# A fused attention and bilinear feed-forward kernel: first weights by narrower columns, first batch's units in another order

## The chip, the cores and the metric

The kernel runs on one core of a Trainium2 chip. The metric is the device time of one execution in microseconds (us), the median of several runs. The profile is one execution recorded by the hardware profiler, which names for every instruction its engine, its line, its tiles, its start and its length.

## What is computed

Attention over 32 memory slots per head, then a feed-forward layer without a nonlinearity, in which two projections are multiplied element by element:

```
# q, k, v: 8 x 8 x 576 x 64 (batch, head, token, dim); phi: 8 x 8 x 576 x 32
a      = softmax(phi over the tokens)
k_m    = einsum('bhsm,bhsd->bhmd', a, k)      # 32 x 64 per head
v_m    = einsum('bhsm,bhsd->bhmd', a, v)
attn   = softmax(q @ k_m.T / 8 over the 32 slots) @ v_m
x      = attn, heads side by side             # 4608 tokens x 512
out    = ((x @ w_a) * (x @ w_b)) @ w_out      # w_a, w_b: 512 x 1536, w_out: 1536 x 512
```

All inputs and the output are float32 in memory. The kernel computes in float16 with float32 accumulation.

## The kernel before

The kernel never forms `x`. It multiplies v_m into the weights first (a **fold**: `vab` = v_m @ w_a and v_m @ w_b, per batch), and then multiplies the attention weights `A` (8 heads x 32 slots = 256 rows, as two groups g of 128, over 576 tokens) by `vab`. An **up** of one block i of 128 features and one half of the tokens (288) is `up_half`: two matmuls for `pa` (line 593, x = 0), evicted by ScalarE into `a_sb` (line 601), and two for `pb`, which VectorE multiplies by `a_sb` into `ht` (line 604). A **down** multiplies `ht` by `w_out` (line 390 for the first four token blocks, afterwards two token blocks at a time with seven products on sums of blocks, line 465, whose weight sums GpSimd forms in `sum_weights`).

The schedule is written out by hand. `units(b)` gives for each batch b a dictionary of named steps, and strings list the order in which they are issued; every engine then works through its own instructions in that order. The names that matter:

- `exp0 exp1`: exp of phi on ScalarE, two halves. `qt0` to `qt3`: transposes of q on VectorE, line 204.
- `ks0 ks1`: sums of k over the tokens on TensorE (line 256), by group, with a normalised copy on VectorE; `vs0 vs1` the same for v; `kt`, `vt`: their transposes (line 274, copy at 277).
- `s0 s1`: scores (line 293); `e0 e1`: their exp (line 306); `den0 den1`: denominators as a product with block-wise ones (line 315) and Ln on ScalarE (line 316), in two token halves; `nr0 nr1`: exp(-Ln) and the multiply into `A` (lines 324, 326).
- `v0a x0a`: a fold of 512 columns with `w_a` (line 338) and its casts to float16 (line 350, one by ScalarE, one by VectorE); `v0b x0b` the same with `w_b`; `hv..`, `hx..`: the same with 256 columns.
- `a3`, `b3`: ups of feature block 3 (`pa`, `pb`), both token halves; `a3.0` only the first half.
- `y3`: three steps of the early downs (`early_downs`: 48 products of 512 columns; four token blocks by thirds of the 12 feature blocks). `f4`: four products of a zero tile (`fill`, line 151) of 256 columns; their result is used by nobody, they keep TensorE at work.
- `-`: nothing; `L`: the loads of the batch after next; a prime: the next batch; an underscore: the batch before.

`chain(0, ...)` at lines 682 to 685 is the first batch's attention and ups, `chain(1, ...)` (line 686) the second batch's attention with early downs between its steps. The later batches run from `slots` strings: one entry after each half of an up step.

All loads but that of the first k go out on GpSimd's queue (software descriptors) and are cast to float16 on the way, except phi and the first k. A load on this queue waits until the eighth before it has landed, so GpSimd stands in the issue order; the transfers follow in that order. The order before is: phi, q (two halves) and v of batch 0, `w_a` and `w_b` in three blocks of 512 columns each, first third of `w_out`, phi, k and half of q of batch 1, second third of `w_out`, the other half of q, v in two halves, last third of `w_out`, and then batches 2 to 4.

Of the kernel before, what the change touches and what calls it, by code (L numbers as in the profile page):

```python
# [8 lines left out]
F32 = mybir.dt.float32  # L9
# [4 lines left out]
P = 128  # L14
CS = 16.0
# [3 lines left out]
def kernel(  # L19
# [11 lines left out]
    nc = tc.nc  # L31

    B, H, S, D = q.shape
# [4 lines left out]
    NFF = d_ff // P  # L38
# [8 lines left out]
    small = ctx.enter_context(tc.tile_pool(name="small", bufs=2))  # L47
# [26 lines left out]
    kv_sbs = [consts.tile([P, 3, NHP, NI * D], F16, name=f"kv_sb{t}") for t in range(2)]  # L74

    def load_phi(b):
        phis[b] = inp.tile([P, NHP, NI * M], F32, name="phi_sb")
        nc.gpsimd.dma_start(out=phis[b], in_=rows(phi, b))

    def load_k(b, hps=slice(0, NHP)):  # L80
        kvs[b] = kv_sbs[b % 2]
        nc.gpsimd.dma_start(out=kvs[b][:, 0, hps], in_=rows(k, b)[:, hps])

    def load_v(b, hps=slice(0, NHP)):
        nc.gpsimd.dma_start(out=kvs[b][:, 1, hps], in_=rows(v, b)[:, hps])

    def load_q(b, hps=slice(0, NHP)):
        if b not in qs:
            qs[b] = inp.tile([P, NHP, NI * D], F16, name="q_sb")
        nc.gpsimd.dma_start(out=qs[b][:, hps], in_=rows(q, b)[:, hps])  # L90

    def load(b):
        load_phi(b)
        load_k(b)
        load_v(b)
        load_q(b)

    def load_wab(lo, hi):
        nc.gpsimd.dma_start(out=wa_sb[:, :, lo:hi], in_=wa_rows[:, :, lo:hi])
        nc.gpsimd.dma_start(out=wb_sb[:, :, lo:hi], in_=wb_rows[:, :, lo:hi])  # L100

    def load_wo(n):
        sl = slice(4 * n, 4 * (n + 1))
        nc.gpsimd.dma_start(out=wo_sb[:, sl, :], in_=wo_rows[:, sl, :])


# [2 lines left out]
    halves = [slice(0, 2), slice(2, 4)]  # L109
# [37 lines left out]
    def fill(n, cols=512):  # L147

        pw = banks.tile([P, 512], F32, name="pw")
        for _ in range(n):  # L150
            nc.tensor.matmul(pw[:, :cols], warm[:, :P], warm[:, :cols], start=True, stop=True)  # L151
# [3 lines left out]
    nc.vector.memset(kv_sbs[0][:, 2], 1.0 / CS)  # L155
    for x in halves:
        nc.vector.tensor_copy(out=kvs[0][:, 0, x], in_=k_f32[:, x])
    load_wab(0, 512)

    ones = consts.tile([P, 4, 32], F16, name="ones")  # L160
    nc.vector.memset(ones, 1.0)
# [2 lines left out]
    nc.gpsimd.affine_select(out=ones, in_=ones, compare_op=ALU.is_ge, fill=0.0, base=31,  # L164
                            pattern=[[32, 4], [0, 32]], channel_multiplier=-1)
    load_wab(512, 1024)
    load_wab(1024, 1536)
    load_wo(0)
    load_phi(1)
    load_k(1)  # L170
    load_q(1, halves[0])
    load_wo(1)
    load_q(1, halves[1])
    for x in halves:
        load_v(1, x)
    load_wo(2)
    nc.gpsimd.memset(kv_sbs[1][:, 2], 1.0 / CS)

    attn = {}
    vabs = {}  # L180
# [6 lines left out]
    def units(b):  # L187

        u = {}
        t = {}  # L190
# [115 lines left out]
                nc.scalar.activation(out=Ev[:, g, :, z, :], in_=pss, func=AF.Exp, scale=1.0 / (8.0 * CS))  # L306
                banks.free(bank)

        def denominators(g):

            t["L", g] = small.tile([P, S], F32, name="L")
            for hf in range(2):
                sl = slice(HALF * hf, HALF * (hf + 1))
                pD = banks.tile([P, HALF], F32, name="pD")
                nc.tensor.matmul(pD, ones, t["E"][:, g, sl], start=True, stop=True)  # L315
                nc.scalar.activation(out=t["L", g][:, sl], in_=pD, func=AF.Ln)  # L316
# [36 lines left out]
        def one(f, *a):  # L353
            return lambda: f(*a)

        for z in range(2):
            u[f"exp{z}"] = one(exp_phi, z)
            u[f"ks{z}"] = one(sums, z, 0)
            u[f"kt{z}"] = one(transpose, z, 0)
            u[f"vs{z}"] = one(sums, z, 1)  # L360
            u[f"vt{z}"] = one(transpose, z, 1)
            u[f"s{z}"] = one(scores, (z,))
            u[f"e{z}"] = one(exp_scores, z)
            u[f"den{z}"] = one(denominators, z)
            u[f"nr{z}"] = one(normalise, z)
            for hf in range(2):
                u[f"nr{z}{hf}"] = one(normalise, z, slice(hf, hf + 1))
            for n in range(NCH):
                u[f"v{n}{'ab'[z]}"] = one(fold, 512 * n, 512 * (n + 1), (z,))
                u[f"x{n}{'ab'[z]}"] = one(take_fold, 512 * n, 512 * (n + 1), z)  # L370
            for n in range(2):
                u[f"hv{n}{'ab'[z]}"] = one(fold, 256 * n, 256 * (n + 1), (z,))
                u[f"hx{n}{'ab'[z]}"] = one(take_fold, 256 * n, 256 * (n + 1), z)
# [13 lines left out]
    def down_part(po, bank, cidx, lo, hi):  # L387
        pair, c = divmod(cidx, NI)
        for i in range(lo, hi):
            nc.tensor.matmul(po, ht[:, i, P * c:P * (c + 1)], wo_sb[:, i, :],  # L390
                             start=(i == 0), stop=(i == NFF - 1))
            if i == NFF - 1:
                banks.free(bank)
                o_sb = opool.tile([P, d_model], F32, name="o_sb")
                nc.scalar.mul(out=o_sb, in_=po, mul=1.0 / (CS * CS))
                for z in range(2):
                    slot = 2 * c + z
                    nc.sync.dma_start(out=out_rows[2 * pair + slot // NI, slot % NI],
                                      in_=o_sb[64 * z:64 * z + 64, :])
            yield  # L400
# [8 lines left out]
    def early_downs():  # L409

        pos = [banks.take([P, d_model], F32, "po", hold=True) for c in range(EARLY)]
        for n in range(3):
            for c in range(EARLY):
                yield from down_part(*pos[c], c, 4 * n, 4 * (n + 1))

# [197 lines left out]
    def ups(steps, side=()):  # L615

        side = iter(side)
        for step in steps:
            for _ in up(*step):
                work.advance()  # L620
                next(side, us[step[0]]["-"])()
        for f in side:
            work.advance()
            f()

    def steps(b, lo, hi):

        return [(b, i, (0, 1)) for i in range(lo, hi)]

    def half_steps(b, hf, lo=0):  # L630

        return [(b, i, (hf,)) for i in range(lo, NFF)]
# [10 lines left out]
    def slots(b, names):  # L643

        def both(fs):
            return lambda: [f() for f in fs]
        def unit(n):
            if n == "fin":
                return lambda: work.pull(-work.done % NFF)
            if n == "L":  # L650
                return lambda: load(b + 2) if b + 2 < B else None
            if n[0] == "y":
                return lambda: some(int(n[1:]))
            if n[0] == "d" and n[1:].isdigit():
                return lambda: work.pull(int(n[1:]))
            return us[b + n.endswith("'") - n.endswith("_")][n.rstrip("'_")]

        return [both([unit(n) for n in x.split("+")]) for x in names.split()]
# [3 lines left out]
    def some(n):  # L662
        for _ in range(n):
            next(early, None)

    def chain(b, plan):


        for x in plan.split():
            if x[0] == "f":  # L670
                fill(int(x[1:]), 256)
            elif x[0] == "y":
                some(int(x[1:]))
            elif x[0] in "ab":
                i, _, hf = x[1:].partition(".")
                for h in ([int(hf)] if hf else (0, 1)):
                    up_half(b, int(i), h, "ab".index(x[0]))
            else:
                us[b][x]()

    fill(16)
    chain(0, "exp0 exp1 qt0 qt1 f12 ks0 f4 kt0 f2 ks1 f1 s0 e0 kt1 qt2 qt3 f2 den0 f4 s1 e1 nr0 f8 vs0 vs1 den1 f2 vt0 vt1 nr1 f4")
    chain(0, "v0a x0a f4 a0 a1 v0b x0b f4 b0 b1 a2 b2 v1a x1a a3 b3 a4 a5 v1b x1b a6 a7 b4 b5 v2a x2a b6 b7 a8 a9")
    load(2)
    chain(0, "v2b x2b a10 a11 b8 b9 b10 b11")
    chain(1, "exp0 y1 exp1 y11 ks0 ks1 y1 qt0 y3 kt0 qt1 s0 e0 kt1 y6 qt2 qt3 den0 y3 s1 nr0 y4 vs0 e1 vs1 den1 y1 vt1 y2 vt0 nr1 hv0a hx0a hv0b y2 hx0b y3")
    load(3)
    sum_weights()
    ups(steps(1, 0, 4), slots(1, "- hv1a+hx1a hv1b+hx1b+y1 - v1a+x1a y3+v1b x1b y3"))
    ups(half_steps(1, 0, 4), slots(1, "- v2a+x2a+v2b+x2b+qt0' - - qt1'+exp0'+qt2' exp1' - kv'+km'+y9"))  # L690
    work.plan(S + HALF, 10)
    ups(half_steps(1, 1, 4), slots(2, "qt3 kvt - sc+e0+e1 - den0+den1+nr0 - v0+nr1+x0a x0b - v1+x1b x1a"))
    second = "v2_+x2a_+exp0 x2b_ exp1 - kv+km qt0 kvt+qt1 - qt2+qt3 sc+e0 e1+v0+x0a den0+x0b nr0+v1+x1a L x1b+exp0' - exp1' v2+x2a den1+qt0' x2b - nr1+qt1'+kv'+km' - - qt2'+kvt'+qt3'"
    every = "- sc+e0 e1 den0 v0+x0a+x0b - - nr0+exp0' - - v1+x1a qt0' x1b+den1 exp1' - v2+x2a+x2b nr1+qt1' kv'+km' qt2' - qt3' - kvt'+L -"
    last = "sc+e0 - e1 - v0+x0b - x0a den1 - - den0 v1+x1b x1a+nr0 - - - - nr1+v2+x2a - - - - - x2b"
    for b in range(2, B):
# [37 lines left out]
```

The softmax here doesn't subtract the row's maximum and nothing guards it: scores larger than these inputs give would overflow.

## Time and profile before

| | |
|---|---|
| time, median of 3 runs | 244.36 us (243.72 to 244.43) |
| profiled span | 241.9 us, granted clock 0.998 |
| busy: VectorE, ScalarE, GpSimd | 167.1, 157.0, 155.9 us |
| loads and stores | 34.12 MB in 24660 packets, mean 141 GB/s |
| exp of phi of batch 0 starts | 7.72 us |
| last up of batch 0 ends, first down starts | 34.4 us |
| first up of batch 1 starts | 48.44 us |

The profile's page gives for each engine the busy time and its share of the span, and then the span in 40 slices of about 6 us, each with a digit for the busy share in tenths. For a stretch of the span, the profile can list the busy time of TensorE (PE), its weight loads (PEld), VectorE (DVE), ScalarE (ACT) and GpSimd (POOL), each with the count of instructions, and then the granted TensorE clock, the DMA share and the GB/s moved. In the timeline each row is one group of like instructions: start, length, engine, line, what it writes and reads, how many, and in square brackets how long the engine stood idle before it and what ended that. In the list of loads the last number is the time from issue to landing.

### The profile page before, as it was taken

The page shows a single profiled execution, that of the slowest core. Times are in us where ns is not written, and L with a number is a line of the kernel's source. Part 1 is how long each engine was busy: PE and PEld are TensorE (multiplying, and loading weights), DVE is VectorE, ACT ScalarE, POOL GpSimd, SP SyncE. Part 2 cuts the span into 40 slices and gives each one's busy share as a digit, 9 for nine tenths or more (in the row PEclk, how much of TensorE's full clock was granted, in tenths as well). Part 3 has the DMA queues.
Part 4 walks back from the last instruction along what each step waited for, and adds up shares of the span by engine and source line. Part 5 has one row for each costly group of instructions (what it writes and reads, how often), then busy time and mean ns, then how long its engine had stood idle before and what let it go on. Part 6 is the DMA issues. An engine that isn't in the chain of part 4 may idle for free.

```text
span 241.9 us, 7661 instructions
## 1 busy us (share of the span) xinstructions
PE 232.9 (96%) x3043; PEld 167.8 (69%) x3043; DVE 167.1 (69%) x402; ACT 157.0 (65%) x406; POOL 155.9 (64%) x130
## 2 busy tenths in 40 slices
PE   7889999999999999999999999999999999999993
PEld 2555664356757867777788777877787878888882
DVE  4536784478858868976984659875987586756642
ACT  2265761679597599598757777587856877465430
POOL 7822354499879549873989759882939087936001
PEclk9999999999999999999999999999999999999999
DMA  6999999999948938962279632795210303033154
GB/s 232 236 206 207 208 255 208 259 223 281 221 98 187 219 81 170 239 117 44 46 176 210 143 87 56 176 205 136 49 43 13 80 13 76 12 80 67 40 128 118
DMA packets 24660, 34.12 MB, mean 141 GB/s; under 512 B 1936, under 2 KB 18704, under 8 KB 24624
## 3 DMA queue, kind: packets, MB, share of 16 engines
q0 software_dynamic: 18160, 23.14, 51.1%
q1 hardware_dynamic: 5952, 9.70, 15.8%
q10 hardware_dynamic: 512, 0.79, 1.0%
q8 instruction: 24, 0.39, 0.6%
q14 instruction: 12, 0.10, 0.1%
HBM read 42.47 MB, written 9.44 MB: 215 GB/s over the span
## 4 chain that ended last, share of the span: by engine, by line
PE 88%; ACT 3%; DMA 3%; DVE 2%; issue 1%; POOL 0%; DVEq 0%; POOLq 0%
PE pa L593 20%; PE pb L593 19%; PE py L465 17%; PE pv L465 8%; PE pva L338 5%; PE po L390 5%; PE px L465 4%; DMA q_sb<-in_q_dram 3%; PE pkv L213 2%; PE pscore L293 2%; PE pD L315 2%; PE pk L256 1%; ACT E L306 1%; PE pT L242 1%; PE pw L151 1%
## 5 line engine op out<-in xcount | busy, mean ns | idle before, releaser
L604 DVE TENSOR_TENSOR ht<-a_sb,pb 128x288 f16<-128x288 f16 x168 | 73.2, 448 | 37.8 <-ACT a_sb L601 28.6
L593 PEld LDWEIGHTS <-vab 128*128 128x128 f16 x768 | 71.7, 98 | 27.1 <-issue 9.4
L601 ACT CAST a_sb<-pa 128x288 f16<-128x288 f32 x168 | 66.7, 408 | 26.0 <-PE pa L593 24.6
L593 PE MATMUL pa<-A,vab 128*128 128x288 f16 x384 | 75.8, 287 | 0.4 <-ACT vab L350 0.2
L593 PE MATMUL pb<-A,vab 128*128 128x288 f16 x384 | 75.0, 286 | 0.3 <-ACT vab L350 0.3
L447 POOL TENSOR_TENSOR h_sums<-ht 128x768 f16<-128x768 f16 x28 | 45.9, 1642 | 33.1 <-DVE ht L604 32.5
L465 PEld LDWEIGHTS <-h_sums 128*128 128x128 f16 x384 | 37.4, 98 | 7.0 <-issue 0.5
L350 DVE CAST vab<-pva 128x512 f16<-128x512 f32 (+1 forms) x50 | 32.3, 663 | 3.2 <-PE pva L338 2.6
L350 ACT CAST vab<-pva 128x512 f16<-128x512 f32 (+1 forms) x50 | 28.0, 585 | 8.6 <-PE pva L338 8.4
L465 PEld LDWEIGHTS <-ht 128*128 128x128 f16 x288 | 28.2, 98 | 5.6 <-issue 0.4
L465 PE MATMUL py<-w_sums,h_sums 128*128 128x256 f16 x192 | 30.4, 272 | 0.0
L447 POOL TENSOR_TENSOR h_sums<-ht,h_sums 128x768 f16<-128x768 f16 x14 | 23.0, 1642 | 1.0
L447 POOL TENSOR_TENSOR h_sums<-h_sums,ht 128x768 f16<-128x768 f16 x14 | 23.0, 1640 | 0.9
L306 ACT ACTIVATE E<-pscore 128x288 f16<-128x288 f32 x32 | 11.4, 418 | 13.7 <-PE pscore L293 13.7
L326 POOL TENSOR_TENSOR A<-E,R 128x576 f16<-128x576 f16 x12 | 15.3, 1276 | 7.4 <-ACT R L324 7.1
L465 PE MATMUL pv<-w_sums,h_sums 128*128 128x256 f16 x96 | 16.2, 273 | 0.0
L465 PE MATMUL py<-wo_sb,ht 128*128 128x256 f16 x96 | 16.0, 273 | 0.0
L472 ACT ACTIVATE u<-py 128x256 f32<-128x256 f32 x32 | 12.6, 392 | 5.0 <-PE py L465 4.8
L204 DVE STREAM_TRANSPOSE qT<-q_sb 128x288 f32<-128x288 f32 x32 | 14.4, 463 | 1.8 <-DMA q_sb<-in_q_dram 1.8
L465 PE MATMUL py<-w_sums,ht 128*128 128x256 f16 x96 | 15.5, 272 | 0.1
L465 PE MATMUL px<-wo_sb,ht 128*128 128x256 f16 x96 | 15.4, 273 | 0.0
L316 ACT ACTIVATE L<-pD 128x288 f32<-128x288 f32 x32 | 11.4, 424 | 4.7 <-PE pD L315 4.3
(65 smaller groups left out, 273.2 us busy)
## 6 DMA issues: line engine op xcount, KB each, us to landing
out_dram<-o_sb SPq DMA_DIRECT2D x68, 128.0 KB, 2.4
phi_sb<-in_phi_dram POOLq DMA_DIRECT2D x8, 576.0 KB, 5.6
kv_sb<-in_v_dram POOLq DMA_DIRECT2D x7, 576.0 KB, 10.1
kv_sb<-in_k_dram POOLq DMA_DIRECT2D x7, 576.0 KB, 7.4
q_sb<-in_q_dram POOLq DMA_DIRECT2D x6, 576.0 KB, 13.4
wa_sb<-in_moe_w_a_dram POOLq DMA_DIRECT2D x3, 512.0 KB, 13.3
wb_sb<-in_moe_w_b_dram POOLq DMA_DIRECT2D x3, 512.0 KB, 15.1
wo_sb<-in_moe_w_out_dram POOLq DMA_DIRECT2D x3, 512.0 KB, 18.1
```

The lines of the kernel that those rows point to most:

```text
L204: nc.vector.transpose(out=t["qT"][:, hp, :].bitcast(F32), in_=qs[b][:, hp, :].bitcast(F32))
L306: nc.scalar.activation(out=Ev[:, g, :, z, :], in_=pss, func=AF.Exp, scale=1.0 / (8.0 * CS))
L326: engine.tensor_tensor(out=attn[b][:, g, sl], in0=t["E"][:, g, sl], in1=t["R", g][:, sl], op=ALU.mult)
L338: nc.tensor.matmul(t["pva", lo, z][g][0][32 * j:32 * j + 32, 0:hi - lo], t["kvT"][64 * r:64 * r + 64, 4 + g, M * j:M * j + M], w_sbs[z][64 ...
L350: engine_copy(out=vabs[b][z][:, g, lo:hi], in_=pva[:, 0:hi - lo])
L390: nc.tensor.matmul(po, ht[:, i, P * c:P * (c + 1)], wo_sb[:, i, :], start=(i == 0), stop=(i == NFF - 1))
L447: engine.tensor_tensor(out=out, in0=in0, in1=in1, op=op)
L465: nc.tensor.matmul(po, lhs[:, i], rhs[:, i], start=first and i == 0, stop=i == KH - 1, skip_group_check=not first)
L472: nc.scalar.mul(out=x, in_=po, mul=scale)
L593: nc.tensor.matmul(ps, vabs[b][x][:, g, P * i:P * (i + 1)], attn[b][:, g, HALF * hf:HALF * (hf + 1)], start=(g == 0), stop=(g == 1))
L601: nc.scalar.copy(out=a_sbs[b, i, hf], in_=ps)
L604: nc.vector.tensor_tensor(out=ht[:, i, t0:t0 + HALF], in0=a_sbs.pop((b, i, hf)), in1=ps, op=ALU.mult)
```

## The change

The change touches only the start, up to the third batch. It has six parts.

1. The first 512 columns of `w_a` and `w_b` are loaded in two blocks of 256 columns, in the order a, b, a, b, so that the first folds can be taken by 256 columns (`hv0a` and so on) as soon as their part is there.
2. The memset of a constant block beside the second batch's k and v moves up on GpSimd, before the last block of `w_a`.
3. `w_out` is loaded in six blocks of two feature blocks each instead of three of four. The order of the loads stays, with each third as two blocks. The early downs follow: sixths instead of thirds.
4. In the first batch's chain both key sums stand together, the q transposes come later, and denominators and normalisation go by halves of the tokens (`den00`, `nr00`), so that the first ups of one half (`a0.0 a1.0`) can start before the other half is ready.
5. The filler products have 128 columns instead of 256 or 512, and there are 114 of them instead of 63.
6. In the second batch's chain, in the slots behind it and in the `second` string, units stand in other places.

```diff
     def load_wo(n):
-        sl = slice(4 * n, 4 * (n + 1))
+        sl = slice(2 * n, 2 * (n + 1))
...
-    load_wab(0, 512)
+    load_wab(0, 256)
+    load_wab(256, 512)
...
     load_wab(512, 1024)
+    nc.gpsimd.memset(kv_sbs[1][:, 2], 1.0 / CS)
     load_wab(1024, 1536)
...
+    for x in "o0 o1 p k q0 o2 o3 q1 v0 v1 o4 o5".split():
+        loads[x]()
...
-        def denominators(g):
+        def denominators(g, hfs=range(2)):
...
-            for hf in range(2):
+            for hf in hfs:
...
+                u[f"den{z}{hf}"] = one(denominators, z, (hf,))
...
-        for n in range(3):
+        for n in range(NFF // 2):
             for c in range(EARLY):
-                yield from down_part(*pos[c], c, 4 * n, 4 * (n + 1))
+                yield from down_part(*pos[c], c, 2 * n, 2 * (n + 1))
...
             if x[0] == "f":
-                fill(int(x[1:]), 256)
+                fill(int(x[1:]), P)
...
-    fill(16)
-    chain(0, "exp0 exp1 qt0 qt1 f12 ks0 f4 kt0 f2 ks1 f1 s0 e0 kt1 qt2 qt3 f2 den0 f4 s1 e1 nr0 f8 vs0 vs1 den1 f2 vt0 vt1 nr1 f4")
-    chain(0, "v0a x0a f4 a0 a1 v0b x0b f4 b0 b1 a2 b2 v1a x1a a3 b3 a4 a5 v1b x1b a6 a7 b4 b5 v2a x2a b6 b7 a8 a9")
-    load(2)
-    chain(0, "v2b x2b a10 a11 b8 b9 b10 b11")
-    chain(1, "exp0 y1 exp1 y11 ks0 ks1 y1 qt0 y3 kt0 qt1 s0 e0 kt1 y6 qt2 qt3 den0 y3 s1 nr0 y4 vs0 e1 vs1 den1 y1 vt1 y2 vt0 nr1 hv0a hx0a hv0b y2 hx0b y3")
+    fill(64, P)
+    chain(0, "exp0 exp1 f18 ks0 ks1 f4 kt0 qt0 qt1 f2 kt1 f4 qt2 qt3 f2 s0 e0 f2 den00 s1 e1 f8 den10 nr00 nr10 vs0 vs1 den01 den11 nr01 f4 vt0 vt1 hv0a nr11 hx0a f6 a0.0 a1.0 hv0b hx0b a0.1 a1.1 hv1a hx1a b0 b1 a3 hv1b a2 hx1b v1a x1a b2 b3 a4 a5 v1b x1b a6 a7 b4 b5 v2a x2a b6 b7 a8 a9 L v2b x2b a10 a11 b8 b9 b11 b10")
+    chain(1, "exp0 y3 exp1 y8 ks0 y1 qt0 y2 kt0 y2 qt1 s0 ks1 y3 e0 y1 kt1 qt2 y1 qt3 den0 y3 s1 y1 nr0 y4 vs0 e1 vs1 y1 den1 y2 vt0 vt1 nr1 y2 hv0a hx0a hv0b y1 hx0b y2")
...
-    ups(steps(1, 0, 4), slots(1, "- hv1a+hx1a hv1b+hx1b+y1 - v1a+x1a y3+v1b x1b y3"))
-    ups(half_steps(1, 0, 4), slots(1, "- v2a+x2a+v2b+x2b+qt0' - - qt1'+exp0'+qt2' exp1' - kv'+km'+y9"))
+    ups(steps(1, 0, 4), slots(1, "- y1+hv1a+hx1a hv1b+hx1b - y3+v1a+x1a y3+v1b+x1b - -"))
+    ups(half_steps(1, 0, 4), slots(1, "- v2a+x2a+v2b+x2b+qt0' - - qt1'+exp0' exp1'+qt2' - kv'+km'+y9"))
...
-    second = "v2_+x2a_+exp0 x2b_ exp1 - kv+km qt0 kvt+qt1 - qt2+qt3 sc+e0 e1+v0+x0a den0+x0b nr0+v1+x1a L x1b+exp0' - exp1' v2+x2a den1+qt0' x2b - nr1+qt1'+kv'+km' - - qt2'+kvt'+qt3'"
+    second = "v2_+x2a_+exp0 x2b_ exp1 - kv+km qt0 kvt+qt1 - qt2+qt3 sc+e0 e1+v0+x0a+x0b den0 nr0+v1+x1a - x1b+exp0' L exp1' v2+x2a den1+qt0'+qt1' x2b - qt2'+nr1+kv'+km' - - kvt'+qt3'"
```

In the last group of lines nothing is added or removed but the places of `x0b`, `L` and q transposes. The kernel computes the same thing with the same numbers of real matmuls, casts and multiplies of the ups; denominators and normalisation of batch 0, two folds of batch 0 and the loads named above are cut finer.

## The prediction

> **What bounds the kernel now.** I read the busy shares and the slices first, then the stretches one by one, then the landing times of the loads, because the change touches only the first quarter of the span.
>
> ```profile
> PE 232.9 (96%) x3043; PEld 167.8 (69%) x3043; DVE 167.1 (69%) x402; ACT 157.0 (65%) x406; POOL 155.9 (64%) x130
> ...
> PE   7889999999999999999999999999999999999993
> ...
> DMA  6999999999948938962279632795210303033154
> ```
>
> TensorE is the bound over the whole span, but the DMA row shows a second full resource: from slice 2 to slice 11 (6 us each) the engines stand at 90% or more. So in the first 66 us two resources are full, and the question is which one ends last there. The stretches (PE busy first, DMA share and GB/s last):
>
> ```profile
> 8.46:19.40 10.94, 9.23 (x244) 5.38 (x244) 5.31 (x17) 5.21 (x12) 5.10 (x7) 1.00 1.23 207
> 19.40:34.40 15.00, 14.69 (x140) 9.68 (x141) 10.78 (x25) 11.23 (x31) 5.80 (x7) 1.00 1.22 227
> 34.40:47.00 12.60, 11.79 (x238) 5.34 (x235) 6.20 (x21) 4.33 (x11) 5.71 (x8) 1.00 1.21 226
> 47.00:60.00 13.00, 12.95 (x138) 7.45 (x139) 9.92 (x24) 10.32 (x27) 12.28 (x9) 1.00 1.17 252
> ```
>
> The busy time of TensorE includes filler. The zero products of line 151 are 28 before 8.46 us and 35 after it; at 0.11 to 0.12 us for 256 columns those 35 hold about 4 us, and they stand where the engine would wait. The loads come at about 207 GB/s as written in float16 (twice that as read in float32) in every stretch, so nothing lands earlier than its place in the queue. Landing is the issue on GpSimd plus the time to landing, for instance:
>
> ```profile
> 29.62 0.70 POOL L85 DMA_DIRECT2D kv_sb<-in_v_dram  x1 [1.87 <-DMA wb_sb<-in_moe_w_b_dram]
> ...
> kv_sb<-in_v_dram POOLq DMA_DIRECT2D x1, 288.0 KB, 15.0
> ```
>
> so the second half of v of batch 1 lands at 44.6 us. Worked out alike: v of batch 0 13.2; the three column blocks of wa and wb 16.6, 19.15, 21.6, 24.2, 26.7, 29.35; first third of wo 31.9; then phi 33.3, k 36.1, q 37.6, second third of wo 40.1, q 41.5, v 43.3 and 44.6, last third of wo 47.2. And what TensorE does there:
>
> ```profile
> 18.95 0.30 PE L593 MATMUL pa<-A,vab 128*128 128x288 f16 x1 [0.16 <-ACT vab L350]
> ...
> 34.38 2.75 PE L390 MATMUL po<-wo_sb,ht 128*128 128x512 f16 x12
> ...
> 44.29 0.87 PE L256 MATMUL pk<-kv_sb,exp_sb 64*32 64x64 f16 x72
> 45.16 0.42 PE L315 MATMUL pD<-E,ones 128*128 128x288 f16 x2
> ```
>
> The first up product starts at 18.95, the first chain ends at 34.4, and the v sums of batch 1, 72 products, run from 44.29 to 45.16. Their second half (from about 44.7) needs the v that landed at 44.6: TensorE and the loads arrive together, within 0.1 us. This is the reading the forecast rests on.
>
> **What the Trainium skill says.** "DMA: Bandwidth & Descriptors", section Specifications, puts full rate at runs of 512 B or more: the new weight pieces have 256 columns, exactly 512 B in float16. Its section "Why small descriptors are slow" gives about 3 cycles of overhead per packet beside 32 B a cycle: two runs of 1 KB take 70 cycles where one of 2 KB takes 67, an estimate of 4.5%. No row of before shows 256 columns. "TensorE: Matmul & The Clock Gate", Part 1, has half clock until some 3.4 us of work and again after an idle window of that length; the trace agrees with the start (512 columns come 0.40 to 0.43 us apart until about 4.7 us, then 0.21) and has no such idle.
>
> **The change part by part.**
>
> Filler at the start. 16x512 and 12x256 columns become 82x128. Cold, a quarter of 0.42 is 0.106 us, so 32 of them take 3.4 us, to 4.7; warm, the nearest row is the transpose of line 242 (128 columns with a new weight load), 6 in 0.34 us, 0.056 each, so 50 take 2.8: end at 7.5 instead of 8.24. The first real product waits for exp of phi (8.35) in both, so 0.
>
> First chain, before the weights. Both key sums stand together, q transposes move behind them on VectorE, denominators go by token halves, fewer and shorter fills (32 of 128 columns for 35 of 256). Following it: key sums to 9.5, transposed keys by 10.3, q transposes 11.1 and 12.2, scores of the first group about 11.5 (before 11.62), second 12.3 to 12.7 (before 13.64), exponentials on ScalarE 0.35 each to about 15.0, v sums 13.9 to 14.9, or 15.5 if the 0.67 us of "issue" idle seen there at 15.6 returns.
>
> First weights by 256 columns. wa's first half should land at about 15.3, wb's at 16.6, then 17.9 and 19.2. The first up product needs wa's half, one fold (0.17) and a cast of 256 columns: 16.6 instead of 18.95, 2.3 us earlier.
>
> Ups of chain 0. 96 products of 0.1225 us and the folds total 13.8 us. After 16.6 they soon catch the loads: four half folds and the ups of f-blocks 0 to 3 are done at about 20.3, while the next wa lands at 21.6 (idle 1.3). Then each fold waits about 0.3 us, and the last, wb at 29.35, sets the end: fold 0.34, a10 and a11 0.98, b8 to b11 1.96, so 32.65. The chain ends 1.9 us earlier, and the front gain of 2.3 is already load-bound.
>
> Chain 1. Loads stand in the same order (o, o, p, k, q, o, o, q, v, v, o, o), and the same bytes precede v. TensorE has 29 down products (0.217 each, 6.3), key sums 0.95, transposes 0.46, scores 0.8, one denominator pair 0.25, first v sums 0.43: 9.2 us of work between 32.65 and 44.6, 12 us. It waits 2.7 us in pieces (k at 36.1, q at 37.6 and 41.5, v). None is 3.4 us long, so I price cold clock at 0. Splitting wo brings its parts up to 1.3 us earlier, but only 32 down products can precede the fifth part (45.9), and 29 are used. So the **1.9 us are turned into waits**.
>
> From v on. The weight pieces delay what is behind them by 0 at least; at most by what rows of 1,152 B lose to rows of 2,304 B in the uncast loads (376 against about 430 GB/s, 13% of 5.1 us, 0.65). I take 0.2, the 4.5% of that page. v sums then end at 44.6+0.2+0.45 = 45.25, before 45.16: +0.1. From there to the first up product of batch 1 before took 3.28 us: 8 down products, a denominator pair, transposes and folds, 2.66 us, and 0.6 of stalls (0.33 at line 338 on kvT). The new order puts one or two down products in each hole; the other chain (pD, two Ln of 0.35, exp 0.65, multiply 0.46, cast 0.4) allows about 2.95 after the v sums: 48.2 instead of 48.44, -0.25.
>
> Slots of batch 1 and second. Down products are moved ahead of folds and one q transpose one slot later; in before ups stand 0.2 us at 58.6 behind a VectorE cast. I take -0.2, between 0 and -0.9 (the stalls of 48.4 to 60.4, 12.0 us for 11.1 of work). The moves in `second` touch stretches where PE shows 24.92 of 25 us: 0.
>
> GpSimd. Five more issues of 0.76 us and the memset (2.04) before the last wa. Behind it on its queue stand only loads, each waiting for the eighth before it; the delayed pieces are issued by 15 us and move after 24. Hidden by the queue: 0. The sums of wo start where they did.
>
> Sum: -0.25 - 0.2, so 244.36 - 0.45 = **243.9**.
>
> **The rivals.**
>
> A, the front gain survives: v is not what ends chain 1, or comes earlier than I work out. For it: no PE wait on a v load is named in the profile. Against it: 44.6 in a queue never short of work. It gives 1.9: 242.5. A smaller form, C: the stalls up to 60 us go too (0.9 with the 0.25): 243.2.
>
> B, slower: the split pieces cost 0.65, all of it ahead of v, and pieces of idle bring the half clock back for part of a window (1 us of work at half rate, +0.5), with nothing gained later: 244.36+0.65-0.25+0.5 = 245.25. For it: TensorE now waits on loads throughout; against it: no idle as long as a window.
>
> **How the numbers follow.** Forecast 0.42, of which 0.08 lies beyond 0.3% (under 243.63); A 0.20; C 0.14; B 0.24. Faster 0.42, within 0.34, slower 0.24. The range leaves out part of A and the end of B: 242.7 to 245.2.
>
> **What would show it.** Right: first up product near 16.6, end of the first chain near 32.7, several waits of TensorE on loads between 32 and 45 (k, q, v), v sums ending within 0.3 us of 45.16, first up of batch 1 near 48.2. Wrong: v landing well before 44.6 (A), or after 45.2, or a lower granted clock between 36 and 50 us (B).

## The result, and the profile after

The kernel after takes **243.3 us** (median; 243.16 to 243.67), the kernel before 244.12 beside it on the same chip; the ratio is 0.997, with a 95% interval of 0.9949 to 0.9991. Measured again, longer, it was 243.47 against 243.94: 0.9986 (0.9973 to 0.9998). The forecast was 243.9, 0.45 us under the kernel before; measured are 0.82 and 0.47 us under it. Single executions of nearly all these kernels take 15 us more, for a reason that comes below; the ratios leave them out, the medians do not.

The two profiled executions show nothing of the gain: 243.64 us before, 243.67 after, both with a span of 241.9. Neither is typical: that of before lies 0.3 us under the median of its longer series, that of the kernel after at the top of its four. So the profile is good for where the time went, stage by stage, and the medians for how much. The page after, in the rows shown of before:

```profile
PE 230.9 (95%) x3110; PEld 169.8 (70%) x3110; DVE 167.2 (69%) x406; ACT 157.2 (65%) x410; POOL 159.4 (66%) x135
...
PE   7769999999999999999999999999999999999993
...
DMA  6999999999947943992269542795220303032154
```

Two us less of TensorE work are not speed but shorter zero products (114 of them take 9.2 us, the 63 of before took 12.5): its second and third slices (6 to 18 us) went from 8 tenths each to 7 and 6. The same stretches as before (TensorE's busy time first, DMA share and GB/s last):

```profile
8.46:19.40 10.94, 7.96 (x247) 5.11 (x248) 5.07 (x19) 5.52 (x15) 7.62 (x10) 1.00 1.34 203
19.40:34.40 15.00, 14.08 (x147) 8.79 (x145) 10.38 (x25) 10.93 (x32) 5.45 (x8) 1.00 1.22 226
34.40:47.00 12.60, 12.59 (x244) 5.99 (x242) 6.73 (x22) 4.38 (x12) 5.86 (x9) 1.00 1.22 221
47.00:60.00 13.00, 12.93 (x136) 7.17 (x135) 10.02 (x26) 10.32 (x27) 12.42 (x10) 1.00 1.17 249
```

From 8.46 to 19.4 TensorE now idles 3 us. From 34.4 to 47 it does not wait at all (12.59 of 12.60; before 11.79). The loads come at 203 GB/s instead of 207 in the first of them. TensorE's timeline at the marks of the prediction (line numbers are one higher than before in this part):

```profile
15.22 0.27 PE L151 MATMUL pw<-warm 128*128 128x128 f16 x2 [1.00 <-issue]
...
19.11 0.66 PE L594 MATMUL pa<-A,vab 128*128 128x288 f16 x4
...
35.01 2.54 PE L391 MATMUL po<-wo_sb,ht 128*128 128x512 f16 x11
...
44.88 0.77 PE L255 MATMUL pk<-kv_sb,exp_sb 64*32 64x64 f16 x72
...
48.34 0.65 PE L594 MATMUL pa<-A,vab 128*128 128x288 f16 x4
```

The first up product came at 19.11, not at 16.6; the first chain ended at 35.01, not at 32.65, and so later than before (34.38). The chain after it made that up, in 13.33 us instead of 14.06: first up of batch 1 at 48.34, before 48.44. VectorE, ahead of the first up:

```profile
16.43 0.64 DVE L326 TENSOR_TENSOR A<-E,R 128x288 f16<-128x288 f16 x2 [3.67 <-ACT R L324]
16.99 0.47 DVE L265 TENSOR_SCALAR kvm<-pk,rphi 128x64 f16<-128x64 f32 x2
...
17.92 0.35 DVE L276 COPY kvT<-pT 128x128 f16<-128x128 f16 x2
```

The v sums had ended at about 16.3, but their copies (line 265) stand behind the multiplies into `A` of the new half-token order, and these had waited for ScalarE.

### The profile page after: what moved, and what is told of

It reads as the page before. It is cut to its first block, busy times and chain, and to the rows that moved or that the text cites. A ratio compares the mean times of both kernels' runs of the same rounds, so it can differ in the third digit from the quotient of the medians.

```text
span 241.9 us, 7803 instructions
## 1 busy us (share of the span) xinstructions
PE 230.9 (95%) x3110; PEld 169.8 (70%) x3110; DVE 167.2 (69%) x406; ACT 157.2 (65%) x410; POOL 159.4 (66%) x135
## 4 chain that ended last, share of the span: by engine, by line
PE 88%; ACT 4%; DMA 3%; DVE 2%; issue 2%; DVEq 0%; POOLq 0%
PE pa L594 20%; PE pb L594 19%; PE py L466 17%; PE pv L466 8%; PE pva L338 5%; PE po L391 5%; PE px L466 4%; DMA phi_sb<-in_phi_dram 3%; PE pkv L212 2%; PE pscore L292 2%; PE pD L315 1%; PE pk L255 1%; ACT E L305 1%; ACT L L316 1%; PE pw L151 1%
## 5 line engine op out<-in xcount | busy, mean ns | idle before, releaser
L326 POOL TENSOR_TENSOR A<-E,R 128x576 f16<-128x576 f16 x12 | 15.3, 1279 | 7.5 <-ACT R L324 7.4
L305 ACT ACTIVATE E<-pscore 128x288 f16<-128x288 f32 x32 | 11.4, 417 | 12.3 <-PE pscore L292 12.2
L466 PE MATMUL px<-wo_sb,ht 128*128 128x256 f16 x96 | 15.4, 273 | 0.0
L194 ACT ACTIVATE exp_sb<-phi_sb 128x576 f16<-128x576 f32 x16 | 11.0, 705 | 5.6 <-DMA phi_sb<-in_phi_dram 5.6
## 6 DMA issues: line engine op xcount, KB each, us to landing
wa_sb<-in_moe_w_a_dram POOLq DMA_DIRECT2D x2, 512.0 KB, 13.8
```

Of the source, the lines that this page charges most:

```text
L326: engine.tensor_tensor(out=attn[b][:, g, sl], in0=t["E"][:, g, sl], in1=t["R", g][:, sl], op=ALU.mult)
L466: nc.tensor.matmul(po, lhs[:, i], rhs[:, i], start=first and i == 0, stop=i == KH - 1, skip_group_check=not first)
```

## The experiments

Two accounts were set against each other from the start. In the first, the loads of k, q and v of batch 1 end the second chain, so that a faster front is waited away, and what gain there is comes from the new order behind it. In the second, the gain is in the front. Later a third was added: the slots are the repair of what the early downs by sixths cost. A mark is the time at which a product starts in the trace; each comes with the measured median, that of the kernel before in the same series, and the ratio with its interval.

**The kernel after once more (again).** No edit.

> The changed kernel itself, again. Both theories give what was measured, 243.3 us, 0.8 under before (ratio 0.997). Its second profile tells which parts of the first belong to the kernel and which to that one execution: the phi load that landed 0.5 us later (8.2 us) and the 1.0 us of idle time at 14.2 us between two zero products. If the kernel owns the idle time it comes back at the same product, the 223rd.

243.47 against 243.94, ratio 0.9986 (0.9973 to 0.9998). The first and third quarter of its executions (without those 15 us longer) end at 243.36 and 243.81; those of the kernel before at 243.65 and 244.43. The gain is 0.3 us at the one and 0.6 at the other. The profile, of an execution that took 258.94 us, shows one more thing. In it phi was as early as before (first key sum at 8.45), yet the first chain ended at 35.62. The stretches (the number after the bracketed counts is the granted clock):

```profile
15.00:16.00 1.00, 1.00 (x74) 0.88 (x74) 0.09 (x1) 0.86 (x3) 0.69 (x2) 0.61 1.44 194
16.00:19.00 3.00, 2.39 (x28) 1.54 (x29) 2.13 (x9) 1.95 (x6) 1.72 (x3) 0.50 1.40 203
19.00:22.00 3.00, 3.00 (x28) 1.27 (x26) 0.42 (x1) 1.89 (x5) 0.91 (x2) 0.50 1.24 204
```

TensorE ran at half clock from about 15.4 to 22 us; four `pa` products took 1.17 us there instead of 0.66. From the first key sum on, no idle stretch before it is longer than 0.98 us. But TensorE was busy for only 1.02 of the 2 us from 13 to 15. From 12 to 15.3 it is busy for 1.75 of 3.30 us here, for 3.12 in the profile of before, but also for only 1.73 in the first profile of the kernel after, which kept the full clock. So the little work may be needed for the fall of the clock, but did not bring it by itself. The prediction priced the half clock at nothing in the second chain, because no idle there reached 3.4 us, and did not name it for the front.

**The front alone (front_only).** Parts 1, 2, 4 and 5 of the change; the rest as before.

```diff
-    load_wab(0, 512)
+    load_wab(0, 256)
+    load_wab(256, 512)
...
-    fill(16)
...
+    fill(64, P)
+    chain(0, "exp0 exp1 f18 ks0 ks1 f4 kt0 ...
```

> The front of the change alone: weights by 256 columns, memset, first chain, short fills; loads of w_out by thirds, second chain, slots and the second string as before. Theory 1 (the v load of the second batch, landing at 44.6 us or a little later, ends the second chain): nothing gained, 244.1 to 244.5, ratio 1.000 to 1.002. Theory 2 (some of the front gain survives): 243.3 to 243.6, ratio 0.997 to 0.998.

243.98 against 243.94, ratio 0.9999 (0.998 to 1.0017). Its first up came at 18.83, the end of the first chain at 34.75, the first up of batch 1 at 48.81 (before 18.95, 34.38, 48.44): the front brings nothing to the median. In its trace it is not early either, so this run can't tell what an early front would bring.

**All but the front (rest_only).** Parts 3 and 6; the memset stays behind the loads.

```diff
-    load_wo(0)
...
+    for x in "o0 o1 p k q0 o2 o3 q1 v0 v1 o4 o5".split():
+        loads[x]()
     nc.gpsimd.memset(kv_sbs[1][:, 2], 1.0 / CS)
...
-    chain(1, "exp0 y1 exp1 y11 ...
+    chain(1, "exp0 y3 exp1 y8 ks0 y1 ...
```

> The rest of the change alone: w_out in six loads, second chain, slots and second string as after; weights by 512 columns, first chain and fills as before. Theory 1: the whole gain, 243.2 to 243.5, and by 0.2 less than that since the loads are not split, ratio 0.996 to 0.998. Theory 2: nothing, 244.0 to 244.3.

260.64 against 243.94, ratio 1.0677 (1.0633 to 1.072), in every execution. Two things went wrong. The memset ended at 39.3 only, because the issue of the sixth `wo` block ahead of it waits for k until 36.59, and the key sums waited 1.95 us for it. That moved the chain so far that VectorE met GpSimd. GpSimd and VectorE at 50.5 us, behind GpSimd's issue of q at 49.72:

```profile
50.47 1.65 POOL L430 TENSOR_TENSOR w_sums<-wo_sb 128x768 f16<-128x768 f16 x1
...
50.59 12.96 DVE L324 TENSOR_TENSOR A<-E,R 128x576 f16<-128x576 f16 x1 [0.36 <-ACT R L322]
```

The multiply into `A`, 0.46 us elsewhere, lasts 12.96, until GpSimd's eight sums of `wo` (1.6 each) are over. In the profile of "again" it is the same: the multiply began at 48.20, inside the q issue of 47.88, and lasted 13.51. In the first profile of the kernel after it began at 47.59, before that issue, and took 0.46: "again" was 0.61 us later there, which moved the multiply into the issue. The Trainium skill, "SBUF — State Buffer", section "Who interferes with whom", says that a VectorE instruction with two SBUF inputs contends with a GpSimd instruction that reads SBUF, and, of VectorE's modes that use both port pairs, that the one issued first has the shared pair for the whole instruction while the other fully blocks. The trace agrees on the block, though the section counts this kind of multiply in no such mode; but it lasted for eight instructions, not for one.

**Fewer zero products (fewer_fills).** The kernel after, with the 64 zero products of 128 columns at its start put back to the 16 of 512 columns of before: as much time, 48 products fewer.

```diff
-    fill(64, P)
+    fill(16)
     chain(0, "exp0 exp1 f18 ks0 ks1 ...
```

> The changed kernel with its first 64 zero products of 128 columns put back to 16 of 512, so 48 products fewer at the start and the same columns. In both profiles TensorE stands idle after its 223rd product (0.67 us in before, 1.0 in after), with no engine to wait for. If this belongs to the count of instructions (their fetch), it moves 48 real products later, out of the fills before the denominators and into the v sums or the folds, and the first up starts 0 to 1 us earlier; if it belongs to the place, it stays in the fills. On the time theory 1 says no change from the changed kernel (243.3), theory 2 up to 1.0 us less (242.3 to 243.0).

243.63 against 243.94, ratio 0.9979 (0.9965 to 0.9993). This is the run that makes the front early:

```profile
33.68 2.54 PE L391 MATMUL po<-wo_sb,ht 128*128 128x512 f16 x11
36.70 0.68 PE L255 MATMUL pk<-kv_sb,exp_sb 64*32 64x128 f16 x36 [0.48 <-DMA kv_sb<-in_k_dram]
...
42.95 0.80 PE L292 MATMUL pscore<-qT,kvT 32*32 32x288 f16 x16 [0.35 <-DVE qT L203]
...
44.87 0.78 PE L255 MATMUL pk<-kv_sb,exp_sb 64*32 64x64 f16 x72
```

The first chain ends 1.33 us earlier than in the kernel after (33.68 for 35.01), and the v sums start at 44.87 instead of 44.88. TensorE waits for k, and then for VectorE, which waits for q:

```profile
42.42 0.84 DVE L203 STREAM_TRANSPOSE qT<-q_sb 128x288 f32<-128x288 f32 x2 [0.69 <-DMA q_sb<-in_q_dram]
```

So a faster front is turned into waits on loads, as the first account has it. Behind that the two traces agree to 0.01 us. That they agree so closely is in part chance: the second half of q landed at 42.4 here (issue at 30.06 and 12.3 us), at 41.8 in both traces of the kernel after. The medians don't depend on that, and this kernel's is no lower than that of the kernel after (243.47).

**The rest with the memset early (rest_early).** As rest_only, with the memset where the kernel after has it.

```diff
     load_wab(512, 1024)
+    nc.gpsimd.memset(kv_sbs[1][:, 2], 1.0 / CS)
     load_wab(1024, 1536)
```

> The rest of the change without its front, now with the memset of the second batch's constant block ahead of the last weight block (at its old place behind the loads it ended at 39.3 us and the k sums waited 1.95 us for it). Weights by 512 columns, first chain and fills as before. Theory 1 (second chain and slots give the gain, the split of the weights costs some of it): the gain of the whole change and 0.2 to 0.4 us more, ratio 0.995 to 0.997, 242.8 to 243.3 us. Theory 2 (front and rest are needed together): no gain, ratio 0.999 to 1.001.

243.55 against 244.2, ratio 0.9976 (0.9955 to 0.9998). First up of batch 1 at 47.69, last store block written by VectorE at 237.19 instead of 237.82. With the old front, parts 2, 3 and 6 are 0.63 us ahead at the end of the trace. (The first chain ended at 34.11 in this execution, 0.27 earlier than in before; rest_guard, below, has the same lead without that.)

**The weights split, nothing else (split_only).**

```diff
-    load_wab(0, 512)
+    load_wab(0, 256)
+    load_wab(256, 512)
```

> The kernel before with one edit: the first 512 columns of both up weights in two loads of 256 columns each. The folds still take 512 columns, so nothing can start earlier. My prediction priced this at 0.2 us, between 0 and 0.65, paid by everything behind it in the load queue. Theory 1 (loads bound the second chain): 0.2 to 0.4 us slower than before, ratio 1.001 to 1.002, and the v of the second batch lands that much later. Theory 2 (TensorE alone bounds it): no change, ratio 1.000.

243.89 against 244.2, ratio 0.9994 (0.9981 to 1.0006). The marks from the end of the first chain on are those of before to 0.01 us (34.38, v sums 44.30, first up 48.45). The loads do come later: GpSimd's waits for the first and the last block of `w_b` end at 19.59 and 29.88 instead of 19.44 and 29.62, and VectorE waits 0.76 us for q until 41.84, before 0.45 until 41.51. TensorE's schedule had that much room.

**The second chain and downs by sixths, old slots (chain1_only).** As rest_early, but the `slots` and `second` strings of before.

```diff
-    chain(1, "exp0 y1 exp1 y11 ...
+    chain(1, "exp0 y3 exp1 y8 ks0 y1 ...
...
     ups(steps(1, 0, 4), slots(1, "- hv1a+hx1a hv1b+hx1b+y1 - v1a+x1a y3+v1b x1b y3"))
```

> The rest with the early memset, but the slots of the second batch and the second string as before: what is left of the change is the second chain's order, w_out in six loads and the place of the memset. My prediction gave the chain 0.25 us and the slots 0.2. If so: ratio 0.998 to 0.999, 243.5 to 243.7 us, and the first up of batch 1 earlier than in before by 0.2 to 0.5 us. If the slots carry it all: no change from before.

245.25 against 244.2, ratio 1.0046 (1.0029 to 1.0063): slower. First up of batch 1 at 47.71, as early as in rest_early (47.69), but:

```profile
54.60 0.71 PE L591 MATMUL pb<-A,vab 128*128 128x288 f16 x4 [0.24 <-ACT a_sb L599]
...
61.08 0.26 PE L211 MATMUL pkv<-kv_sb,exp_sb 64*32 64x192 f16 x4
61.57 0.65 PE L211 MATMUL pkv<-kv_sb,exp_sb 64*32 64x192 f16 x41 [0.23 <-DVE ht L602]
```

The k and v sums of batch 2 start at 61.08, in rest_early at 59.99. So the new slots are needed with downs by sixths: without them the stretch from the first up of batch 1 to these sums takes 13.37 us, with them 12.30, and in before, with thirds and the old slots, 11.99. In the lines, before, then rest_guard (below) for the new slots:

```profile
48.44 0.65 PE L593 MATMUL pa<-A,vab 128*128 128x288 f16 x4
...
60.43 0.96 PE L213 MATMUL pkv<-kv_sb,exp_sb 64*32 64x192 f16 x72
```

```profile
47.70 0.65 PE L591 MATMUL pa<-A,vab 128*128 128x288 f16 x4
...
60.00 1.06 PE L211 MATMUL pkv<-kv_sb,exp_sb 64*32 64x192 f16 x72
```

**No load of k (no_k).** fewer_fills, with batch 1's k not loaded but set to a constant; that part of the result is left out.

```diff
+    nc.gpsimd.memset(kv_sbs[1][:, 0], 1.0 / CS)
+    kvs[1] = kv_sbs[1]
...
-    for x in "o0 o1 p k q0 o2 o3 q1 v0 v1 o4 o5".split():
+    for x in "o0 o1 p q0 o2 o3 q1 v0 v1 o4 o5".split():
...
-    fill(64, P)
+    fill(16)
```

> The changed kernel with 16 fills of 512 columns (its first chain ended at 33.7 us, 1.3 us before the changed kernel's, and nothing came of it), and without the load of the second batch's k: a constant stands in its place, so that part of the result is left out. 1.2 MB fewer are read ahead of q, w_out and v, which then land 2.8 us earlier. Theory 1 (loads hold the second chain): the front's gain comes through, v sums start 0.8 to 1.3 us earlier than 44.87 and the time is 242.3 to 242.8. Theory 2 (something on TensorE or a short chain between the engines holds it): v sums again near 44.9 and 243.4 to 243.7.

257.08 against 244.2, ratio 1.0531 (1.0489 to 1.0574), in every execution: the multiply into `A` began at 46.10, 0.1 us after GpSimd's sums (45.99), and again lasted 12.96 us. But the v sums before it stood at 43.39, in fewer_fills at 44.87.

**The same with a guard (no_k_guard).** A multiply of the last 8 columns of batch 1's `A` on GpSimd stands before its sums, so that these can't begin before VectorE has written `A`.

```diff
+    guard = consts.tile([P, 8], F16, name="guard")
+    last = attn[1][:, 1, S - 8:S]
+    nc.gpsimd.tensor_tensor(out=guard, in0=last, in1=last, op=ALU.mult)
     sum_weights()
```

> The kernel without the load of the second batch's k (a constant in its place, so that part of the result is left out), with one thing added: GpSimd, before the sums of w_out, multiplies 8 columns of the second batch's A, so it can't begin the sums before VectorE has written A. In no_k the first up stood at 46.86 us, 1.5 us earlier than 48.34, and then VectorE's multiply into A (start 46.10) lasted 13 us, as long as the eight sums of w_out on GpSimd that had begun at 45.99. Theory 1 (the loads hold the second chain, and the 13 us are that collision): 242.0 to 242.5 us, no execution above 250. If the 13 us had another cause: 256 to 258 again.

242.46 against 243.81, ratio 0.9944 (0.9924 to 0.9963). All six executions lie between 242.34 and 242.94, those of no_k between 255.93 and 258.5. TensorE's marks:

```profile
33.81 2.54 PE L393 MATMUL po<-wo_sb,ht 128*128 128x512 f16 x11
...
43.67 0.78 PE L257 MATMUL pk<-kv_sb,exp_sb 64*32 64x64 f16 x72
...
47.14 0.65 PE L596 MATMUL pa<-A,vab 128*128 128x288 f16 x4
...
59.44 1.06 PE L214 MATMUL pkv<-kv_sb,exp_sb 64*32 64x192 f16 x72
```

The first chain ends 1.20 us before that of the kernel after, and the v sums, the first up of batch 1 and the sums of batch 2 stand 1.20 to 1.21 us before its own: the front's lead comes through whole. In fewer_fills, with the same front and k loaded, none of it did.

**The rest with the guard (rest_guard).** rest_early and the three lines above.

> The rest of the change with the early memset and the front of before, plus the guard: GpSimd's sums of w_out wait for the second batch's A. Theory: the median of rest_early or slightly less (242.9 to 243.6, ratio 0.995 to 0.998), since GpSimd's sums have 0.6 us of idle time behind them and the guard costs about 0.1 us; no execution near 258, of which there were 3 among 22 of the same kernel without the guard. If the guard costs on the path: up to 0.3 us more.

243.63 against 243.81, ratio 0.9992 (0.9973 to 1.0012). GpSimd's timeline at the guard:

```profile
48.40 0.21 POOL L688 TENSOR_TENSOR guard<-A 128x8 f16<-128x8 f16 x1
48.56 3.22 POOL L430 TENSOR_TENSOR w_sums<-wo_sb 128x768 f16<-128x768 f16 x2
```

It costs 0.2 us of GpSimd, and no mark: the first chain ends at 34.37 (before 34.38), first up at 47.70, last block of VectorE at 237.19 as in rest_early. Yet its span is 242.4 us against 241.2: the last stores took that much longer to land. So 0.63 us on the trace is not 0.63 in a median; the landing of the last stores moves by more than that from one execution to the next. Of 56 executions of kernels with the guard none was 15 us longer; without it, 22 of 279 were (both counts without the two kernels where all were). On the chip of the guard's series, though, only 1 of 44 executions of before was, so for the single ones the guard is not shown to help; that it prevents the block is shown by no_k and no_k_guard.

**The first two thirds of the early downs whole, the last one by sixths for two of the four token blocks, with the new slots (downs_new_slots) and the old ones (downs_old_slots).** With loads in six blocks, the second chain's new order, the guard and the memset early, and the front of before; `second` is the new one in both.

```diff
-        for n in range(3):
-            for c in range(EARLY):
-                yield from down_part(*pos[c], c, 4 * n, 4 * (n + 1))
+        parts = [(c, 4 * n, 4 * (n + 1)) for n in range(2) for c in range(EARLY)]
+        parts += [(c, lo, lo + 2) for lo in (8, 10) for c in (0, 1)] + [(c, 8, 12) for c in (2, 3)]
+        for c, lo, hi in parts:
+            yield from down_part(*pos[c], c, lo, hi)
```

> rest_guard with the early downs' 48 products in another order: the first two thirds of the features by fours as in before, the last third as 2, 2, 2, 2, 4, 4, so that two token blocks finish (and free their bank and are evicted by ScalarE) at steps 38 and 40 and two at 44 and 48, where the sixths finish them at 42, 44, 46 and 48. In the changed kernel two evictions of 0.6 us stood together at 53.9, and from the first up of batch 1 to the k and v sums of batch 2 it took 12.30 us against 11.99 in before. Theory 3 (bunched ends of the downs cost those 0.3 us): 0.2 to 0.4 us less than rest_guard, ratio to before 0.994 to 0.997. If the slots are what they should be for sixths: same or up to 0.5 slower.

> The same as downs_new_slots, but with the slots of the second batch as before. In chain1_only the old slots with the downs by sixths took 13.37 us from the first up of batch 1 to the sums of batch 2, where before took 11.99 with the same slots and the downs by thirds. Theory 3 (it is the bunched ends, not the slots): back to 12.0 to 12.2 us, and 242.6 to 243.3 us, ratio 0.994 to 0.997. If the old slots are bad in themselves with the new chain: 244 to 245 us as in chain1_only.

New slots: 243.85 against 243.81, ratio 1.0001 (0.9987 to 1.0016); old slots: 243.49 against 243.81, 0.9983 (0.9971 to 0.9996). From the first up of batch 1 to the sums of batch 2:

| early downs | old slots | new slots |
|---|---|---|
| thirds (before) | 11.99 us | not run |
| two thirds whole, the last partly by sixths | 12.29 us | 12.82 us |
| sixths | 13.37 us | 12.30 us |

The third account holds in one direction: the new slots are better with the downs by sixths and worse with the one other order that was run. What it hoped for, that an order of downs nearer to thirds would win back the 0.3 us with either slots, failed: with the new slots it lost half a microsecond, with the old ones it only equalled the change.

## Why the prediction was right, and where not

The forecast of 243.9 was 0.6 and 0.4 us above the two medians, its direction right. Most of what it named as signs of being right did not come: first up near 16.6 (19.11), end of the first chain near 32.7 (35.01), waits of TensorE on loads between 32 and 45 us (none), v sums ending within 0.3 us of 45.16 (45.58). Only the first up of batch 1, near 48.2, did (48.34). So the number was in good part luck.

Its main thought, that the front's gain is turned into waits on loads, was not put to the test by the change, whose front was not early. The experiments bear it out: fewer_fills (chain 1.33 us earlier, nothing gained behind it) and no_k_guard (k not loaded, and a lead of 1.20 us comes through). Which load holds is less settled. In fewer_fills it is k (0.48 us) and the second half of q (0.69 on VectorE, 0.35 on TensorE) that are waited for, and the v sums after them only stand in line. But that q was late in this execution, and v's second half landed at 44.8 (issue at 32.64 and 12.2 us), where its 36 products began at about 45.2, half of the sums' 0.70 us after 44.87. So had q come earlier, the v that the prediction named would have let the sums come only about 0.4 us sooner, an estimate from these figures.

**The step that failed** is "First chain, before the weights", with what follows in "First weights by 256 columns" and "Ups of chain 0": first up at 16.6 and end at 32.65, measured 19.11 and 35.01. Against 16.6 the trace gives 2.51 us: phi landed 0.49 later in this execution; TensorE idled 1.00 us on "issue" at 14.2 (the prediction left this out of 13.9 and kept it at 0.67 as an alternative); 0.16 more up to the v sums at 15.55; VectorE's multiplies into `A` ahead of the v copies, 0.66 (16.33 to 16.99); and net 0.20 for the rest of the way (copies, transposes, fold, cast). Of these the queue on VectorE was to be read off the unit string: `nr00 nr10` precede `vs0 vs1`, and each engine works in order. From the first up to the end of the chain 15.9 us passed; the prediction had 16.05, but as 13.8 of work and the rest waits on loads. TensorE was busy for 14.98 of them and waited for no load, only 0.41 and 0.48 us for casts: near the right sum from two wrong parts.

The terms of its sum:

- Split of the weights, +0.2 up to v: no time in split_only. The delay is real (0.15 to 0.33 us on the loads) and there was room for it. This agrees with the estimate of 4.5% from "DMA: Bandwidth & Descriptors" in the Trainium skill, section "Why small descriptors are slow": of the 5.1 us of the two blocks that would be 0.23.
- Second chain, -0.25: -0.74 in rest_guard, whose first chain ends with that of before (34.37 and 34.38), three times the term. The v sums end 0.22 earlier (44.94 for 45.16; the prediction had 0.1 later), and from there to the first up 2.76 us pass instead of 3.28, -0.52 (the prediction had 2.95 us).
- Slots, -0.2: +0.31 (12.30 us for 11.99). The missing term is the downs by sixths, which the prediction put at nothing: with the old slots they cost 1.38 us (13.37), and the new slots win back 1.07 of it. Their evictions come in pairs (two ScalarE evictions in 1.09 us at 53.87 where before three single ones of 0.60 were spread from 48.43 to 55.65); that the pairs are the cause is not shown, since downs_new_slots has single ones and takes 12.82.
- `second`, 0: -0.20 (from the sums of batch 2 to the same mark two later: 58.59 us for 58.79).

Together -0.22 - 0.52 + 0.31 - 0.20 = -0.63, which is the lead of 0.63 at the end of rest_guard's trace. The forecast of -0.45 is near it because two errors of half a microsecond nearly cancelled (0.49 in the chain, 0.51 in the slots). In the trace of the kernel after itself the first chain ends 0.63 later than in before, which the same parts then make up: 0.63 - 0.73 + 0.31 - 0.20 = 0.01.

**Memset and issues on GpSimd, 0:** right as the change has them. The memset's move was needed, though: rest_only shows 1.95 us of wait where it stays.

**Rivals A and C.** A, a front gain that survives, did not come: the change had no front gain, and in fewer_fills it was gone at the v sums. C's 243.2 is nearer to the first median than the forecast, but its cause, the stalls up to 60 us gone, is not there: that stretch took 0.31 us longer.

**Rival B,** slower, named the half clock. It does return, in "again" from 15.4 to 22 us, though not where the rival put it (36 to 50 us) and not behind waits on loads, but behind a stretch of little work in the front. The first chain ended 0.61 later there than in the first profile of the kernel after (35.62 for 35.01), with phi half a microsecond earlier, and the first up of batch 1 still stood 0.61 later (48.95 for 48.34). Of the three traces with the new first chain and its 114 zero products (after, "again", front_only) only this one has it; how often it happens can't be told from that.

**What stays open.** The profiled execution of the kernel after is not earlier than before at the end (237.87 and 237.82), while the medians are 0.5 to 0.8 apart; so where the medians' gain arises is not shown. The middle half of the executions lies within 0.45 us in "again", within 0.78 in before and 0.94 in rest_guard, so part of the gain can be fewer late executions; one trace for each kernel doesn't tell. The "issue" idle, 1.00 us in the kernel after, stands after TensorE's 223rd product in every trace here but those of no_k and no_k_guard, whatever that product is: 0.55 to 1.00 us long, in fewer_fills, where it fell amid the v sums, 0.18, and it ends between 14.7 and 16.8 us. It goes with the count of instructions; that it is the fetch of instructions was not shown. No version was shown to beat both kernels: rest_guard leads at every late mark, but its median doesn't.

## What to carry to other kernels

Where two resources end a stage together, work on one of them alone moves its end only into waits: find the load or product that comes last at each join (here k and q, with v close behind) and shorten that. Follow every engine's queue in order before moving a unit ahead, since a multiply that waits for another engine holds the copies behind it. Before a long run of GpSimd operations on SBUF, give its first one a dependency on the last VectorE operation with two SBUF inputs that must not be caught behind it.

## What the hardware showed unexpectedly

A VectorE multiply of two SBUF tiles that began inside a GpSimd issue (at 48.20 in "again") or 0.1 us into the first of eight GpSimd sums (rest_only, no_k) stayed blocked for all eight, about 13 us, not for one of 1.6; in no_k_guard 0.2 us of guard removed it. TensorE's clock fell to half for some 6.6 us without any idle longer than 0.98, after a stretch in which it was a little over half busy. The Trainium skill, "TensorE: Matmul & The Clock Gate", Part 1, puts the return of the half clock down to an idle window of about 3.4 us. In "again" no such window stands before it, so full idleness was not needed there; one execution gives no threshold, and the first profile of the kernel after, as little busy, kept the full clock.
